# Recurrent memory attention on one core: odd heads' scores earlier, value copies by strip halves, token values after the output product

## The chip, the cores and the metric

The kernel runs on one core of one Trainium2 chip. The metric is the device time of one execution in microseconds (us); lower is better. The engines are PE (TensorE: matmuls, and weight loads that overlap them), DVE (VectorE), ACT (ScalarE), POOL (GpSimd) and SP (SyncE, which here only issues DMAs). Each runs its own instructions in program order and waits on semaphores for the others.

## The reference, cut to what matters

A sequence of 2048 rows of 640 is normalised and cut into 64 segments of 32 rows. Eight memory rows go from segment to segment: what attention puts out for them in one segment is the memory of the next. A feed-forward part (640 to 1728, squared relu, back to 640) follows over all rows.

```python
mem = mem0
for s in range(64):
    h = concatenate([mem, xs[s]])              # 8 + 32 rows of 640
    q, k, v = h @ Wq, h @ Wk, h @ Wv           # 32 heads of 128
    scores = where(mask, q @ k.T * 128**-0.5, -1e9)   # memory rows see all, token rows what is before them
    o = softmax(scores) @ v
    o = o @ Wo                                 # back to 640
    mem, out[s] = o[:8], o[8:]
y = x + out
y = y + (relu(layernorm(y) @ w1 + b1) ** 2) @ w2 + b2
```

## The kernel before

The four attention weights stay in SBUF. `step(b, sp)` does segment s = 4b + sp; its main product has 32 rows, namely the 8 memory rows and the first 24 token rows, which stand side by side in `hTall`. The last 8 token rows of each segment ("tails") need no memory, so their q, k and v products are made ahead, four segments at a time, in small units kept in the list `fill`. One unit is 4 matmuls of 128x512 (or, for the tails' output product, some 6 of 128x320). `run(fill, n)` puts n units at a place in PE's order; the calls of `run(fill, ...)` in `step` are where the kernel fills PE's waits.

The order of work is the order of the code, written out by hand; no scheduler moves anything, and the tile framework adds the semaphore waits. A step goes so on PE:

1. q, k, q, k products (`project`, recorded at line 208 as all products of rows are); between the halves ACT evacuates (L224, L226, L399), DVE transposes (L229, L402) and POOL spreads the memory rows' q into `qz` (L369, L371).
2. `scores(0)`: memory rows' scores of the even half of the heads into the tile `sm`, of which there is one buffer; `soft1` takes the maximum (DVE, L421) and the exponential `em` (ACT, L424), `soft2` the reciprocal, the product and the transpose `pTm` (DVE, L430 to L434). "Even" and "odd" stand here for n = 0 and n = 1.
3. First two fifths of the even heads' v product; `token_scores(0)`; the rest, then its copy to `v` (ACT, L500).
4. Two fifths of the odd heads' v product, `scores(1)`, `token_scores(1)`, the rest of the odd v product (copy at L516), one fill unit.
5. `token_values(s - 1)`: probabilities of the segment before times its values for the token rows, 32 + 8 small matmuls (L350, L355) into the first 256 columns of each of the four banks of `po`.
6. `values(0)` and `values(1)`: the memory rows' value products, 16 + 4 matmuls each (L443, L448), into the columns from 256 on; `values_out`: DVE copies n = 0 (L215), ACT n = 1 (L217) into the last 8 columns of each row of `oT`.
7. Row transposes of the coming block where there are any (list `win`, L185), two fill units; softmax of the token scores on DVE, ACT and POOL (L531 to L546).
8. The output product `wo_rounds` into `pw` (L240, 64 matmuls in 16 rounds, over the 8 memory columns of this segment and 24 token columns of segment s - 2), `wo_out` (ACT copy `otmp`, L247, DVE sum `o`, L248), `mem_to_hT` (two DVE transposes into `hTall`, L314): the next step can start.
9. `token_out(s - 1)`: ACT copies the token values to `oT` (L360), POOL keeps the tail rows (L362); the store of s - 2 (SP); five fill units; `tails_in` (POOL, L318); all remaining fill units; the token probabilities' transposes for the next step.

In `po` the first matmul with `start=True` in a bank opens it; the others add, or write where nothing is yet. Head p of `oT` is p = 16 n + 4 g + j, with strip g of the value products in bank g of `po`. A round of the output product takes its rows so:

```python
                    p = h // 8 * 16 + kh * 8 + h % 8      # h is the round, kh = 0, 1
```

Of the kernel before, what the change touches and what calls it, by code (L numbers as in the profile page):

```python
# [16 lines left out]
def kernel(  # L17
# [19 lines left out]
    M = A_mem0.shape[1]  # L37
    SEG = 32
# [4 lines left out]
    DC = D // 128  # L43
# [5 lines left out]
    NK = SEG + M  # L49
# [25 lines left out]
    wv = wts.tile([128, DC * HE], BF16)  # L75
# [19 lines left out]
    for g in range(G):  # L95
        r = slice(32 * g, 32 * g + 32)
# [101 lines left out]
    def proj(w, by, lhs, n, ps, c0, c1):  # L198

        if by == "columns":  # L200
            wr = w[:].rearrange("p (c g j n k e) -> p c n k g j e", c=DC, g=G, n=2, j=4, k=4)
        elif by == "half":
            wr = w[:].rearrange("p (c k j n e) -> p c n k j e", c=DC, k=G, n=2, j=4)
        else:
            wr = w[:].rearrange("p (c k n f) -> p c n k f", c=DC, k=G, n=2)
        for c in range(c0, c1):
            for k in range(4):
                nc.tensor.matmul(ps[32 * k:32 * k + 32, :], lhsT=lhs(c), rhs=wr[:, c, n, k], start=(c == 0), stop=(c == DC - 1))  # L208
# [4 lines left out]
    def evac(dve, out_, in_):  # L213
        if dve:
            nc.vector.tensor_copy(out=out_, in_=in_)  # L215
        else:
            nc.scalar.copy(out=out_, in_=in_)  # L217
# [33 lines left out]
    fill, late, mid, win = [], [], [], []  # L251

    def run(q, n):
        while n > 0 and q:
            q.pop(0)()
            n -= 1
# [78 lines left out]
    def store_main(o, s):  # L335
        for ch in range(2):
            nc.sync.dma_start(out=o_all[s * SEG:s * SEG + HD, ch * DH:(ch + 1) * DH],
                              in_=o[32 * ch:32 * ch + HD, :])

    oTg = oT[:].rearrange("p (n g j) q -> p n g j q", n=2, g=G)  # L340
    back = []

    def token_values(s, v, vt4, po):

        sp = s % 4
        pTk, pTx = back.pop()
        for i in range(HG):
            for g in range(G):
                r = slice(32 * g, 32 * g + 32)
                nc.tensor.matmul(po[:, g, i * 32:(i + 1) * 32], lhsT=v[r, i * E:(i + 1) * E], rhs=pTk[r, i, :],  # L350
                                 start=(i == 0), stop=False, skip_group_check=True)
        for u in range(2):
            for g in range(G):
                r = slice(32 * g, 32 * g + 32)
                nc.tensor.matmul(po[:, g, u * 128:(u + 1) * 128].rearrange("p (j q) -> p j q", q=32)[:, :, 0:TL],  # L355
                                 lhsT=vt4[r, sp, u, :], rhs=pTx[r, u], start=False, stop=True, skip_group_check=True)

    def token_out(s, po):
        for n in range(2):
            nc.scalar.copy(out=oTg[:, n, :, :, 0:SEG],  # L360
                           in_=po[:, :, n * 128:(n + 1) * 128].rearrange("p g (j q) -> p g j q", q=32))
        nc.gpsimd.tensor_copy(out=oTts[s // 4 % 2][:, :, s % 4 * TL:(s % 4 + 1) * TL], in_=oT[:, :, 0:TL])  # L362
# [10 lines left out]
    prev = {}  # L373

    def step(b, sp, v=None):
        s = b * 4 + sp
        last = s == NS - 1
        lhs = rows_of(b, sp)
        ready = v is not None
        if not ready:  # L380
            v = s2.tile([128, EG], BF16, tag="v", name="v")
# [25 lines left out]
        def scores(n):  # L407
            sm = chn.tile([128, 512], F32, tag="ch", name="sm")
            for g in range(G):
                nc.tensor.matmul(sm[32 * g:32 * g + 32, SEG:2 * SEG], lhsT=ident[:, 0:32],  # L410
                                 rhs=bmask[:].rearrange("p j k -> p (j k)"), start=True, stop=False, skip_group_check=True)
            for j in range(4):
                for g in range(G):
                    p = n * 16 + g * 4 + j
                    nc.tensor.matmul(sm[32 * g:32 * g + 32, 0:2 * SEG], lhsT=qz[:, p, :], rhs=kT[:, p, :],  # L415
                                     start=False, stop=(j == 3), skip_group_check=True)
            sms[n] = sm

        def soft1(n):
            mx = s2.tile([128, 1], F32, tag="mx", name="mx")  # L420
            nc.vector.tensor_reduce(out=mx[:], in_=sms[n][:, 0:2 * SEG], op=ALU.max, axis=AX.X, negate=True)  # L421
            em = s2.tile([128, 2 * SEG], BF16, tag="em", name="em")
            zm = s2.tile([128, 1], F32, tag="zm", name="zm")
            nc.scalar.activation(out=em[:], in_=sms[n][:, 0:2 * SEG], func=ACT.Exp, bias=mx[:, 0:1], scale=1.0,  # L424
                                 accum_out=zm[:])
            ems[n], zms[n] = em, zm

        def soft2(n):
            rm = s2.tile([128, 1], F32, tag="rm", name="rm")
            nc.vector.reciprocal(out=rm[:], in_=zms[n][:])  # L430
            pm = s2.tile([128, 2 * SEG], BF16, tag="pmem", name="pmem")
            nc.vector.tensor_scalar(out=pm[:], in0=ems[n][:], scalar1=rm[:, 0:1], scalar2=None, op0=ALU.mult)
            pT = s2.tile([128, 2 * SEG], BF16, tag="pTm", name="pTm")
            nc.vector.transpose(out=pT[:], in_=pm[:])  # L434
            return pT

        def values(n, pT, po):
            c0 = 256 + n * 4 * M
            for j in range(4):
                i = n * 4 + j  # L440
                for g in range(G):
                    r = slice(32 * g, 32 * g + 32)
                    nc.tensor.matmul(po[:, g, c0 + j * M:c0 + (j + 1) * M], lhsT=v[r, i * E:(i + 1) * E],  # L443
                                     rhs=pT[r, j * M:(j + 1) * M], start=(s == 0 and i == 0), stop=False,
                                     skip_group_check=True)
            for g in range(G):
                r = slice(32 * g, 32 * g + 32)
                nc.tensor.matmul(po[:, g, c0:c0 + 4 * M], lhsT=vt4[r, sp, n, :], rhs=pT[r, 32:64],  # L448
                                 start=False, stop=True, skip_group_check=True)

        def values_out(po):
            for n in range(2):
                c0 = 256 + n * 4 * M
                evac(n == 0, oTg[:, n, :, :, SEG:NK], po[:, :, c0:c0 + 4 * M].rearrange("p g (j m) -> p g j m", m=M))

        project("q", wq, qT, 0)
        if not last and not ready:
# [21 lines left out]
        vt4 = vt4s[b]  # L479
# [6 lines left out]
        def token_scores(n):  # L486
            if n == 0:
                for g in range(G):
                    nc.tensor.matmul(skv[32 * g:32 * g + 32, :, M:NK], lhsT=ident[:, 0:32], rhs=mask[:],
                                     start=True, stop=False, skip_group_check=True)  # L490
            for j in range(4):
                for g in range(G):
                    nc.tensor.matmul(skv[32 * g:32 * g + 32, n * 4 + j, :], lhsT=qT[:, n * 16 + g * 4 + j, :],  # L493
                                     rhs=kT[:, n * 16 + g * 4 + j, 0:NK], start=False, stop=(n == 1 and j == 3),
                                     skip_group_check=True)
# [3 lines left out]
            proj(wv, "half", lhs, 0, ps0, 2, DC)  # L499
            nc.scalar.copy(out=v[:, 0:512], in_=ps0[:])  # L500
        if not last:
            pT0 = soft2(0)
        if not ready:
            ps1 = mmtile()
            proj(wv, "half", lhs, 1, ps1, 0, 2)
        if not last:
            scores(1)
        token_scores(1)
        if not ready:
            proj(wv, "half", lhs, 1, ps1, 2, DC)  # L510

        if not last:
            soft1(1)
            pT1 = soft2(1)
        if not ready:
            nc.scalar.copy(out=v[:, 512:1024], in_=ps1[:])  # L516
        run(fill, 10 if ready else 1)
        if ready:
            run(late, 100)
        po = pop.tile([128, G, 512], F32, tag="po", name="po")  # L520
        if s:
            token_values(s - 1, prev["v"], prev["vt4"], po)
        if not last:
            for n, pT in ((0, pT0), (1, pT1)):
                values(n, pT, po)
            values_out(po)
# [24 lines left out]
        o = wo_out(pw)  # L551
        if not last:
            mem_to_hT(o, (s + 1) // 4, (s + 1) % 4)
        if s:
            token_out(s - 1, po)
        if s > 1:
            store_main(o, s - 2)
        if not last:
            run(fill, 5)
            tails_in((s + 1) // 4, (s + 1) % 4)  # L560
        run(mid, 2)
        run(fill, 100)
# [218 lines left out]
    po = pop.tile([128, G, 512], F32, tag="po", name="po")  # L781
# [7 lines left out]
    for t in range(S // NT):  # L789
# [6 lines left out]
        for fc in range(FC):  # L796
            ps = mmtile()
            for c in range(DC):
                if fc < FFULL:
                    nc.tensor.matmul(ps[:], lhsT=w1[:, c, fc * 128:(fc + 1) * 128], rhs=hnT[:, c, :],  # L800
                                     start=(c == 0), stop=(c == DC - 1))
                    continue
                for hh in range(2):
                    nc.tensor.matmul(ps[FREM * hh:FREM * (hh + 1), 0:HT], lhsT=w1[:, c, fc * 128:F],
                                     rhs=hnT[:, c, HT * hh:HT * (hh + 1)], start=(c == 0), stop=(c == DC - 1))
            w = NT if fc < FFULL else HT
            r = rs_[fc % 4]
# [73 lines left out]
```

## Time and profile before

| | us |
|---|---|
| median of 3 runs | 1051.98 (1051.05 to 1052.34) |
| the profiled execution | 1052.44 |
| its span | 1050.6 |
| PE matmul busy | 964.3 |
| DVE busy | 656.6 |
| ACT busy | 536.5 |
| POOL busy | 326.0 |

A row of the timeline gives start, length, engine, line, operation, output and inputs, shape, count and, in brackets, the idle time before it and what ended that. Rows that overlap on PE are pipelined matmuls, whose ends are modelled. A row of the windows view gives a stretch, its length, and for PE, PEld (weight loads), DVE, ACT and POOL the busy time and the count of instructions; then granted clock, DMA share and GB/s.

### The profile page before, as it was taken

To read this page: it belongs to the slowest core of one execution; us is meant where nothing else is said; L and a number is where in the kernel's file an instruction comes from. 1 tells how busy PE (TensorE), PEld (TensorE's weight loads), DVE (VectorE), ACT (ScalarE), POOL (GpSimd) and SP (SyncE) were. 2 spreads that over 40 slices of the span, in tenths; PEclk is the share of its full clock that TensorE was granted. 3 is DMA by queue.
4 is the path that set the end of the run, shared out by engine and by line. 5 is a ranking of instruction groups with operands and counts; after the bars stand their busy time and mean duration, and the time that the engine had idled before them with its cause. 6 is when DMAs were issued, how large, how long until landed. Compare 5 with 4: busy or idle time off the path is not lost.

```text
span 1050.6 us, 56335 instructions
## 1 busy us (share of the span) xinstructions
PE 964.3 (92%) x25671; PEld 562.9 (54%) x25680; DVE 656.6 (62%) x1804; ACT 536.5 (51%) x1225; POOL 326.0 (31%) x866
## 2 busy tenths in 40 slices
PE   4779799989999999999999999999999998899998
PEld 2335456556555555555555555555555554555565
DVE  2245676767676767666767666666676677565442
ACT  2325455556555555555555555555555555534331
POOL 1033333333333323333333333333333333253110
PEclk9979999999999999999999999999999999999999
DMA  8950100000000001000000000000000110512200
GB/s 325 404 185 25 18 10 26 11 21 9 23 17 20 16 14 32 13 21 14 26 14 22 14 26 15 21 14 27 14 21 8 45 33 6 182 59 76 76 26 26
DMA packets 39183, 51.42 MB, mean 49 GB/s; under 512 B 6240, under 2 KB 35040, under 8 KB 37024
## 3 DMA queue, kind: packets, MB, share of 16 engines
q1 hardware_dynamic: 38080, 47.30, 13.6%
q8 instruction: 200, 3.28, 1.3%
q14 instruction: 39, 0.32, 0.1%
q0 software_dynamic: 320, 0.26, 0.1%
q10 hardware_dynamic: 544, 0.26, 0.1%
HBM read 38.37 MB, written 9.44 MB: 46 GB/s over the span
## 4 chain that ended last, share of the span: by engine, by line
PE 75%; DVE 10%; DMA 5%; issue 4%; ACT 4%; POOL 0%; SPq 0%; ACTq 0%; DVEq 0%; POOLq 0%
PE ps L208 41%; PE pw L240 14%; PE y L832 5%; PE ps L800 5%; DVE hTall L314 3%; DVE o L248 3%; DMA xt<-in_A_x_dram 3%; ACT otmp L247 3%; PE po L443 2%; PE sm L415 2%; PE po L350 1%; PE ps L240 1%; PE ps L493 1%; DMA wq<-in_B_w_dram 1%; DMA vt<-vt_d 1%
## 5 line engine op out<-in xcount | busy, mean ns | idle before, releaser
L208 PEld LDWEIGHTS <-hTall 128*32 128x32 bf16 x7680 | 188.6, 96 | 221.1 <-DVE hTall L314 62.4
L208 PE MATMUL ps<-wq,hTall 128*32 128x512 bf16 x2520 | 158.5, 380 | 35.4 <-DVE hTall L314 34.9
L208 PE MATMUL ps<-wv,hTall 128*32 128x512 bf16 x2520 | 170.0, 379 | 0.7 <-ACT v L500 0.7
L240 PE MATMUL pw<-wo,oT 128*32 128x320 bf16 x4224 | 157.4, 300 | 1.9 <-DVE pTt L564 1.2
L208 PE MATMUL ps<-wk,hTall 128*32 128x512 bf16 x2520 | 157.9, 379 | 0.0
L224 ACT ACTIVATE row<-ps 128x512 bf16<-128x512 f32 x156 | 91.9, 601 | 87.0 <-PE ps L208 84.4
L240 PEld LDWEIGHTS <-oT 128*32 128x32 bf16 x4224 | 111.3, 97 | 45.3 <-DVE oT L215 13.7
L543 POOL TENSOR_TENSOR pkt<-ek,rk 128x64 bf16<-128x64 bf16 x64 | 18.8, 294 | 368.0 <-DVE rk L541 368.0
L229 DVE STREAM_TRANSPOSE qT<-row 128x512 bf16<-128x512 bf16 x128 | 90.0, 704 | 48.2 <-ACT row L224 48.1
L226 ACT CAST row<-ps 128x512 bf16<-128x512 f32 x115 | 65.8, 596 | 36.1 <-PE ps L208 36.1
L318 POOL COPY kT<-kTt 128x1024 bf16<-128x1024 bf16 x64 | 74.6, 1165 | 13.7 <-DVE kTt L229 13.7
L208 PEld LDWEIGHTS <-hTt 128*32 128x32 bf16 x1920 | 51.0, 99 | 42.7 <-issue 7.5
L369 POOL COPY qz<-qT 128x96 bf16<-128x96 bf16 x126 | 33.4, 265 | 122.8 <-DVE qT L229 121.7
L360 ACT CAST oT<-po 128x512 bf16<-128x512 f32 x128 | 68.7, 589 | 1.6
L248 DVE TENSOR_TENSOR o<-pw,otmp 64x320 bf16<-64x320 f32 x66 | 31.8, 482 | 60.3 <-ACT otmp L247 60.3
L229 DVE STREAM_TRANSPOSE kT<-row 128x512 bf16<-128x512 bf16 x65 | 46.0, 708 | 29.6 <-ACT row L226 29.6
L247 ACT COPY otmp<-pw 64x320 f32<-64x320 f32 x66 | 27.9, 422 | 69.6 <-PE pw L240 69.5
L832 PE MATMUL y<-wq,wk 128*128 128x320 bf16 x416 | 61.0, 299 | 0.1
L539 DVE TENSOR_REDUCE zk<-ek 128x8 f32<-128x320 bf16 x64 | 31.1, 486 | 41.8 <-ACT ek L535 41.8
L399 ACT CAST row<-ps 128x256 bf16<-128x256 f32 x126 | 40.7, 375 | 29.6 <-PE ps L208 29.6
L535 ACT ACTIVATE ek<-tk 128x320 bf16<-128x320 f32 x64 | 30.1, 471 | 44.6 <-DVE tk L533 44.6
L424 ACT ACTIVATE em<-sm,mx 128x64 bf16<-128x64 f32 x126 | 40.4, 320 | 24.3 <-DVE mx L421 24.3
(113 smaller groups left out, 1656.1 us busy)
## 6 DMA issues: line engine op xcount, KB each, us to landing
wv<-in_A_Wv_dram SPq DMA_DIRECT2D x5, 1024.0 KB
wq<-in_A_Wq_dram SPq DMA_DIRECT2D x5, 1024.0 KB
wk<-in_A_Wk_dram SPq DMA_DIRECT2D x5, 1024.0 KB
wo<-in_A_Wo_dram SPq DMA_DIRECT2D x4, 1280.0 KB
vt<-vt_d SPq DMA_DIRECT2D x60, 64.0 KB
xt<-in_A_x_dram SPq DMA_DIRECT2D x20, 160.0 KB
vt_d<-row SPq DMA_DIRECT2D x22, 128.0 KB
wq<-in_B_w_dram SPq DMA_DIRECT2D x1, 2080.0 KB
```

What stands on the lines that cost most here:

```text
L208: nc.tensor.matmul(ps[32 * k:32 * k + 32, :], lhsT=lhs(c), rhs=wr[:, c, n, k], start=(c == 0), stop=(c == DC - 1))
L224: nc.scalar.mul(out=row, in_=ps, mul=scale)
L226: nc.scalar.copy(out=row, in_=ps)
L229: nc.vector.transpose(out=dst[:, n * 16:(n + 1) * 16, 0:32], in_=row.rearrange("p (h e) -> p h e", e=32))
L240: nc.tensor.matmul(pw[32 * j:32 * j + 32, 0:DH], lhsT=lhs(p), rhs=wov2[:, head(p), ch], start=(h == 0), stop=(h == 15))
L247: nc.scalar.copy(out=tmp[0:64], in_=pw[64:128, 0:DH])
L248: nc.vector.tensor_tensor(out=o[0:64], in0=pw[0:64, 0:DH], in1=tmp[0:64], op=ALU.add)
L318: nc.gpsimd.tensor_copy(out=kT[:, :, SEG:2 * SEG].rearrange("p h (j k) -> p h j k", k=TL), in_=k.unsqueeze(2).to_broadcast([128, H, 4, TL]))
L360: nc.scalar.copy(out=oTg[:, n, :, :, 0:SEG], in_=po[:, :, n * 128:(n + 1) * 128].rearrange("p g (j q) -> p g j q", q=32))
L399: nc.scalar.copy(out=row[:, u * 256:(u + 1) * 256], in_=ps[:, u * 256:(u + 1) * 256])
L800: nc.tensor.matmul(ps[:], lhsT=w1[:, c, fc * 128:(fc + 1) * 128], rhs=hnT[:, c, :], start=(c == 0), stop=(c == DC - 1))
L832: nc.tensor.matmul(y[:, hh, 0:DH], lhsT=f1T[:, fc, k * 128:(k + 1) * 128], rhs=w2[:, fc, cs], start=(fc == 0), stop=False, skip_group_chec ...
```

## The change

- `scores(1)` and `soft1(1)` move up, ahead of the whole odd v product; the even heads' last transpose (`soft3`) goes behind them, `token_scores(1)` follows, and the odd v product runs unbroken.
- Two fill units in place of one stand ahead of the value products.
- `token_values(s - 1)` moves from ahead of the value products to behind the output product, two fill units after it; `token_out(s - 1)` goes behind it, and the store of s - 2 ahead of both. Four fill units follow in place of five. The value products now open the banks of `po` in every step, the token values only in the last.
- `values_out` splits by strips: DVE copies strips 0 and 1 of both n, ACT strips 2 and 3, where before DVE copied n = 0 and ACT n = 1 of all strips.

```diff
-    def token_values(s, v, vt4, po):
+    def token_values(s, v, vt4, po, first=True):
...
-                                 start=(i == 0), stop=False, skip_group_check=True)
+                                 start=(first and i == 0), stop=False, skip_group_check=True)
...
         def soft2(n):
+            return soft3(soft2a(n))
+
+        def soft2a(n):
...
+            return pm
+
+        def soft3(pm):
             pT = s2.tile([128, 2 * SEG], BF16, tag="pTm", name="pTm")
...
-                                     rhs=pT[r, j * M:(j + 1) * M], start=(s == 0 and i == 0), stop=False,
+                                     rhs=pT[r, j * M:(j + 1) * M], start=(i == 0), stop=False,
...
         def values_out(po):
-            for n in range(2):
-                c0 = 256 + n * 4 * M
-                evac(n == 0, oTg[:, n, :, :, SEG:NK], po[:, :, c0:c0 + 4 * M].rearrange("p g (j m) -> p g j m", m=M))
+            for h in range(2):
+                gs = slice(2 * h, 2 * h + 2)
+                evac(h == 0, oTg[:, :, gs, :, SEG:NK],
+                     po[:, gs, 256:256 + 8 * M].rearrange("p g (n j m) -> p n g j m", n=2, m=M))
...
         if not last:
-            pT0 = soft2(0)
+            pm0 = soft2a(0)
+            scores(1)
+            soft1(1)
+            pT0 = soft3(pm0)
+        token_scores(1)
         if not ready:
             ps1 = mmtile()
-            proj(wv, "half", lhs, 1, ps1, 0, 2)
+            proj(wv, "half", lhs, 1, ps1, 0, DC)
         if not last:
-            scores(1)
-        token_scores(1)
-        if not ready:
-            proj(wv, "half", lhs, 1, ps1, 2, DC)
-
-        if not last:
-            soft1(1)
             pT1 = soft2(1)
...
-        run(fill, 10 if ready else 1)
+        run(fill, 10 if ready else 2)
...
-        if s:
+        if last:
             token_values(s - 1, prev["v"], prev["vt4"], po)
-        if not last:
+        else:
             for n, pT in ((0, pT0), (1, pT1)):
                 values(n, pT, po)
             values_out(po)
...
-        if s:
-            token_out(s - 1, po)
         if s > 1:
             store_main(o, s - 2)
+        if s:
+            if not last:
+                run(fill, 2)
+                token_values(s - 1, prev["v"], prev["vt4"], po, False)
+            token_out(s - 1, po)
         if not last:
-            run(fill, 5)
+            run(fill, 4)
             tails_in((s + 1) // 4, (s + 1) % 4)
```

## The prediction

> **What bounds the kernel now.** I read the page first: how full TensorE is, and what the chain that ended last is made of.
>
> ```profile
> span 1050.6 us, 56335 instructions
> ...
> PE 964.3 (92%) x25671; PEld 562.9 (54%) x25680; DVE 656.6 (62%) x1804; ACT 536.5 (51%) x1225; POOL 326.0 (31%) x866
> ...
> q8 instruction: 200, 3.28, 1.3%
> ```
>
> PE is busy 92% of the span, but that share hides a loop: each step's memory output is the next step's input. So I went on to the chain of waits in order of time for two neighbouring steps (start, length, what).
>
> ```profile
> 500.65 4.50 PE ps L208 x80
> ...
> 509.57 2.28 PE pw L240 x64
> ...
> 513.63 4.50 PE ps L208 x80
> ...
> 521.65 0.35 issue
> ...
> 526.93 4.50 PE ps L208 x80
> ```
>
> A step runs from its q product (L208) to the next one's: 12.98 us for the first, 13.30 for the second. Its last part, from the end of the output product (509.57 + 2.28 = 511.85) over otmp, o and the hTall transposes to the next q product, is 1.78 us of ACT and DVE work that no PE order shortens. The rest is PE in program order with a few handovers. The second step holds one thing more, 0.35 us put down to "issue". The third view is the timeline of all engines in the first, clean step.
>
> ```profile
> 505.58 0.27 POOL L369 COPY qz<-qT 128x96 bf16<-128x96 bf16 x1 [1.43 <-DVE qT L229]
> 505.61 0.77 DVE L402 STREAM_TRANSPOSE kT<-row 128x256 bf16<-128x256 bf16 x2
> ...
> 505.76 1.25 PE L208 MATMUL ps<-wv,hTall 128*32 128x512 bf16 x20
> ...
> 505.94 0.21 ACT L424 ACTIVATION_READ_ACCUMULATOR em<-sm,mx 128x1 f32 x1
> ...
> 506.63 0.59 ACT L500 CAST v<-ps 128x512 bf16<-128x512 f32 x1 [0.48 <-PE ps L208]
> ...
> 507.49 0.31 ACT L424 ACTIVATE em<-sm,mx 128x64 bf16<-128x64 f32 x1 [0.27 <-DVE mx L421]
> ...
> 507.98 0.58 ACT L516 CAST v<-ps 128x512 bf16<-128x512 f32 x1
> ...
> 508.09 0.37 PE L350 MATMUL po<-pTk,v 32*128 32x32 bf16 x32
> ...
> 508.38 0.48 PE L443 MATMUL po<-pTm,v 32*128 32x8 bf16 x16
> 508.40 0.25 DVE L434 STREAM_TRANSPOSE pTm<-pmem 128x64 bf16<-128x64 bf16 x1
> ...
> 508.73 0.26 PE L443 MATMUL po<-pTm,v 32*128 32x8 bf16 x16
> ...
> 508.83 0.19 PE L448 MATMUL po<-pTm,vt 32*128 32x32 bf16 x4
> ...
> 509.11 0.29 DVE L215 CAST oT<-po 128x128 bf16<-128x128 f32 x1 [0.46 <-PE po L448]
> ...
> 509.43 0.27 ACT L217 CAST oT<-po 128x128 bf16<-128x128 f32 x1 [0.87 <-DVE oT L215]
> ...
> 509.45 2.36 PE L240 MATMUL pw<-wo,oT 128*32 128x320 bf16 x64
> ...
> 511.64 1.68 PE L208 MATMUL ps<-wq,hTt 128*32 128x512 bf16 x28
> ...
> 512.37 1.07 ACT L360 CAST oT<-po 128x512 bf16<-128x512 f32 x2
> ```
>
> Two handovers stand on the path. The odd heads' value product (the second L443 group) starts at 508.73, 0.08 after the odd pTm is done (508.40 + 0.25 = 508.65); the token value products at 508.09 only fill that wait. And the output product starts at 509.45, 0.05 after the DVE copy of the even heads ends at 509.40; the ACT copy of the odd heads ends later, at 509.70, but the output product's first eight rounds read even heads only, so it hides.
>
> Now the 0.35 us of issue. I asked for counts of PE instructions between such holes, and for the whole steady stretch:
>
> ```profile
> 127.14:844.24 717.09, 680.71 (x20707) 402.74 (x20708) 490.46 (x1370) 402.06 (x963) 237.60 (x679) 1.00 0.07 19
> ```
> ```profile
> 522.00 0.20 PE L448 MATMUL po<-pTm,vt 32*128 32x32 bf16 x4 [0.35 <-issue]
> ```
> ```profile
> 522.00:535.28 13.29, 12.61 (x384) 7.24 (x384) 9.24 (x25) 7.52 (x18) 4.17 (x12) 1.00 0.03 7
> 614.23:627.57 13.35, 12.66 (x384) 7.11 (x384) 9.49 (x26) 7.53 (x18) 4.28 (x12) 1.00 0.03 6
> ```
> ```profile
> 627.58 0.20 PE L443 MATMUL po<-pTm,v 32*128 32x8 bf16 x6 [0.37 <-issue]
> ```
>
> The 54 steps from 127.15 to 844.24 take 717.09 us, 13.28 each. Between one hole and the next stand 384 matmuls and 384 weight loads, 768 = 3 x 256 instructions. Queue q8 brought 3.28 MB in 200 packets; PE's 51,351 instructions over 200 are 257. So a hole is a packet of PE's own instructions that comes late, and it shows only where 256 instructions pass too fast. The fastest 256 are those that end with the value products: 80 of values, 80 of token values, 8 of fill, 24 of v, 32 of token scores, 32 of scores, all from about 506.9 to 508.9: 2.0 us.
>
> What the holes cost: three steps in four are 12.98 without one. Every fourth also transposes x rows ahead of the output product:
>
> ```profile
> 540.18 4.50 PE ps L208 x80
> ...
> 548.53 0.39 PE pt L185 x5
> ...
> 549.46 2.20 PE pw L240 x64
> ...
> 553.46 0.60 PE ps L208 x5
> ```
>
> That is 13.28, with no hole in it. The mean without holes is (3 x 12.98 + 13.28) / 4 = 13.055, so holes take 13.28 - 13.055 = 0.225 us a step, 12 us in 54 steps.
>
> **The change, part by part**, on the clean step's clock.
>
> *Scores ahead of the odd v product.* The same instructions stand between 505.76 and the end of the odd v product, so the latter ends where it did and its ACT copy still ends at 508.56. Moved up by 8 matmuls of the odd v product (20 take 1.08, so 0.43), scores(1) starts at 506.41. Its cover: em of the even heads ends at 506.15, so the one buffer for score tiles is free; the odd kT halves end at 506.38, 0.03 ahead of need, so this cover is thin (gone, it costs what kT is late, some 0.05). em(1) stands behind the v copy on ACT, which ends at 507.22; it starts at about 507.25 instead of 507.49, and pTm(1), 1.16 later (508.65 - 507.49), is done at 508.41. The even pTm, 0.25 on DVE, now waits behind mx(1), and is done long before values(0).
>
> *Token values out of the way, a second fill unit in.* Between the odd v product and values(1), PE loses 32 + 8 token products (508.09 to 508.38, 0.29) and gains one fill unit of 4 matmuls (28 of them run from the output product's end, 511.81, to 513.32, 1.51, so 0.22). PE would be ready at about 508.45 (508.09 + 0.22 + some 0.1 for values(0)), pTm(1) at 508.41; what is late next is the odd v copy, 508.56. values(1) starts at 508.61 (the 0.05 of the oT handover) instead of 508.73: gain 0.12.
>
> *Copies by strip halves.* As built, the ACT copy still waits for the DVE copy in every one of the 63 steps (the rows they write in oT interleave now). And the output product's first round reads strips of both halves (its second weight pair waits for ACT), where before it read the even heads only. So it starts not 0.05 after the DVE copy but 0.05 after the ACT copy: 509.70 - 509.40 = 0.30 later. Queued behind the waiting weight load is all of PE: the loop waits. In the transposing steps PE is busy there until 549.46 anyway, 0.39 longer; the wait hides, and these steps keep most of the 0.12: 13.20.
>
> *Token values behind the output product.* They go into the 1.78 us in which PE waits for hTall. PE work there was 7 units (1.51, idle from 513.32 to 513.63, 0.31); it becomes 6 units and the token products, 1.29 + 0.29 to 0.38, idle 0.1 to 0.2: free, by that idle time (in steps whose units belong to the tail output it is nearly gone; past it up to 0.1 a step). token_out on ACT (1.07) waits now for the token products, some 0.5 later than 512.37, and the oTt and kT copies on POOL follow it; POOL idles 1.43 before its second qz copy, so this hides. The token values' buffer is read 0.5 later too; the next step first writes it at its value products, 7.7 us in (508.38 - 500.65). On SP only the store's place in the program moves, not its order.
>
> A clean step is thus 12.98 - 0.12 + 0.30 = 13.16, slower than before. The mean without holes: (3 x 13.16 + 13.20) / 4 = 13.17.
>
> *The holes.* Taking 80 instructions out of the fast stretch is the gain nobody orders. The fastest 256 now end with the value products and hold 80 of values, 16 of fill, 40 of v, 32 of token scores, 40 of scores, 24 of the even v product and 24 of the first token scores: from about 505.7 to 508.75, 3.1 us instead of 2.0. The packet that came late at 522.00 bounds what is needed:
>
> ```profile
> 518.73:521.99 3.26, 2.92 (x148) 1.71 (x141) 2.04 (x9) 1.99 (x7) 0.51 (x3) 1.00 0.02 5
> ```
>
> That stretch, the 256 instructions ahead of the hole as counted back from it, lasted 3.26 us with the 0.35 of waiting in it. So 3.3 us a packet is surely enough; 3.1 may leave up to 0.2 now and then, where a packet's end falls into the value products (about 80 places of 256). Holes left: 0 to 0.06 a step; I take 0.02. A hole cannot be less than nothing; the upper bound is the 0.225 of today.
>
> Sum: 13.28 - (13.17 + 0.02) = 0.09 us a step, 54 steps, 5 us. The other steps (first, last, feed-forward) I take as unchanged: they wait for DMA or other products. The profiled execution is 1052.44 (span 1050.6), 0.46 above the median 1051.98: 1047 against the median.
>
> **Rivals.**
>
> *A, slower: the holes stay.* If a packet's coming late does not depend on how dense the stretch is, or the new order has stretches as dense for it, the 0.225 stays on top of 13.17: 13.395, +0.115 a step, +6 us, 1058. It decides from holes of about 0.11 a step upwards. For it: packets need up to 3.3 us and my densest stretch is 3.1. Against: all holes I looked at end at the same place of 256 and in the fast stretch. The Trainium skill (Runtime: NRT & Kernel Launch, section Instruction fetch mechanics) gives refills in blocks of 256 instructions fetched while the current one runs, and calls crossing a block mostly hidden. By that rule the holes would be something else, and A the result; the trace agrees on the block's size, and disagrees on hidden, with 0.35 us at 522.00.
>
> *B, much faster: the two copies do run side by side.* Both would end near 509.30 on the new clock, the output product start 0.30 earlier, clean steps come to 12.86; 40 steps x 0.30 = 12 us more: 1035. The built waits speak against it. The Trainium skill (PSUM — Partial Sum Buffer, PSUM bank collisions) has two engines read different banks at once without harm, which is what halves by strip allow; by that rule alone B would hold. No row of before shows it: 509.43 follows 509.40.
>
> *C, slower: the window overfills.* If the token products, or token_out behind them on ACT, hold up the next step's q row by over 0.1 us, a step is 13.3 or more: 1053 to 1060. It decides where PE has no idle left before the q product.
>
> **Chances.** Forecast 0.66, A 0.16, B 0.05, C 0.13. The forecast's own range is 1043 to 1051 (0.07 a step either way). The whole range goes up to A's 1058 and C's middle, and leaves B out: 1042 to 1058. A difference of 0.2%, 2.1 us, is about what a measurement of this kernel can tell. Faster by more: most of the forecast and B, 0.64; within: 0.14; slower: 0.22.
>
> **What would show it.** In the profile after: L217 still released by L215; the output product's weight load waiting for ACT, idle 0.3 before it on PE; values(1) released by the odd v copy; no or few "issue" waits at the value products; PE idle before hTall down to 0.1 or 0.2; clean steps of 13.1 to 13.2, all alike. Wrong: ACT and DVE copies side by side; holes as often as before; q products that wait for anything but hTall.

## The result and the profile after

| | before | after |
|---|---|---|
| median, measured side by side | 1052.16 (1051.05 to 1053.84, 4 runs) | 1044.73 (1044.32 to 1044.90, 4 runs) |
| the profiled execution | 1052.44 | 1044.78 |
| its span | 1050.6 | 1043.0 |

The ratio is 0.9927, with a 95% interval of 0.9910 to 0.9945. The forecast was 1047. Two lines of the page of after come first.

```profile
span 1043.0 us, 56466 instructions
...
PE 986.2 (95%) x25680; PEld 558.0 (54%) x25680; DVE 650.4 (62%) x1804; ACT 530.6 (51%) x1225; POOL 323.4 (31%) x866
```

PE is busier than before (986.2 against 964.3) though it does the same work. The 22 us are not work. Matmul ends are modelled and overlap, so a short wait between two matmuls is covered by the modelled end of the first: the 4224 matmuls of the output product take 300 ns each in both profiles, but as a group they are busy for 157.4 us before and 169.5 after. The rest stands in the groups of the fill units. The next view is the chain of waits in order of time for two neighbouring steps of after.

```profile
497.03 4.50 PE ps L208 x80
...
503.11 0.15 PE ps L500 x16
...
505.87 2.52 PE pw L240 x64
...
510.21 4.50 PE ps L208 x80
...
523.38 1.68 PE ps L208 x25
```

Both steps, from q product to q product, take 13.17 to 13.18. Of the 39 steady steps of before that transpose no rows, the shortest take 12.94 to 12.95; only 11 are within 13.01, and the longest takes 13.73. The 12.98 of the prediction's first step is therefore not quite clean. A clean step became longer by 0.22, and the spread is gone: 38 of the 39 take 13.17 to 13.18. The windows view puts that into sums: first the 54 steady steps (the same steps as in the prediction, which start a little later here and end earlier), then the last four steps.

```profile
127.50:839.79 712.29, 698.90 (x20707) 398.08 (x20707) 486.15 (x1370) 396.88 (x963) 235.28 (x678) 1.00 0.07 19
...
839.79:893.80 54.01, 49.04 (x1503) 29.39 (x1503) 39.80 (x115) 28.72 (x70) 20.37 (x56) 1.00 0.07 19
```

The same last four steps in the windows view of before:

```profile
844.24:901.18 56.94, 49.19 (x1503) 29.83 (x1503) 41.38 (x115) 29.45 (x71) 20.75 (x57) 1.00 0.07 18
```

The 54 steps took 717.09 before and take 712.29, 4.80 less. The last four took 56.94 and take 54.01, 2.93 less. With the start (0.35 longer) and the end (0.3 shorter) that makes the difference between the spans (7.6, or 7.7 before rounding).

The timeline of the first of the two steps shows the handovers.

```profile
504.39 0.58 ACT L520 CAST v<-ps 128x512 bf16<-128x512 f32 x1 [0.48 <-PE ps L208]
504.42 0.25 DVE L440 STREAM_TRANSPOSE pTm<-pmem 128x64 bf16<-128x64 bf16 x1
...
505.03 0.26 PE L449 MATMUL po<-pTm,v 32*128 32x8 bf16 x16
...
505.40 0.29 DVE L215 CAST oT<-po 128x128 bf16<-128x128 f32 x1 [0.73 <-PE po L454]
...
505.72 0.27 ACT L217 CAST oT<-po 128x128 bf16<-128x128 f32 x1 [0.75 <-DVE oT L215]
505.74 0.10 PEld L240 LDWEIGHTS <-oT 128*32 128x32 bf16 x2 [0.37 <-DVE oT L215]
505.75 2.65 PE L240 MATMUL pw<-wo,oT 128*32 128x320 bf16 x64
506.04 2.02 PEld L240 LDWEIGHTS <-oT 128*32 128x32 bf16 x62 [0.20 <-ACT oT L217]
...
508.76 0.37 PE L350 MATMUL po<-pTk,v 32*128 32x32 bf16 x32
508.97 0.24 PE L355 MATMUL po<-pTx,vt 32*128 32x32 bf16 x8
509.14 1.05 PE L208 MATMUL ps<-wq,hTt 128*32 128x512 bf16 x16
509.43 1.07 ACT L360 CAST oT<-po 128x512 bf16<-128x512 f32 x2
...
510.21 0.34 PEld L208 LDWEIGHTS <-hTall 128*32 128x32 bf16 x12 [0.52 <-DVE hTall L314]
```

Counted from the step's q product (497.03): the odd value product starts at 8.00, 0.06 after the odd v copy ends at 504.97 and no longer behind pTm; before it was 8.08 (508.73 - 500.65). The output product loads two weights after the DVE copy, then waits until 506.04, 0.05 after the ACT copy. So the delay does not show as a gap on PE: it shows as a group of 64 matmuls that takes 2.65. It ends at 11.37 (505.75 + 2.65 - 497.03). Before, by the same rows, the group took 2.36 and ended at 11.16 (509.45 + 2.36 - 500.65). The window from there to the next q product is 1.81, before 1.82 (the prediction's 1.78 takes the end from the chain, 511.85). The waits of after, summed over the kernel (us in total, times, longest):

```profile
ACT oT L217 <- DVE oT L215: 50.4, 63, 3.9
...
PEld L240 <- ACT oT L217: 9.4, 47, 0.2
```

47 of 63 steps wait 0.2 for the ACT copy: all but the transposing ones. No wait of a PE matmul is put down to "issue" in this view.

### The profile page after: what moved, and what is told of

It is laid out like the page before. It is cut to its first block, busy times and chain, and to the rows that moved or that the text cites. A ratio compares the mean times of both kernels' runs of the same rounds, so it can differ in the third digit from the quotient of the medians.

```text
span 1043.0 us, 56466 instructions
## 1 busy us (share of the span) xinstructions
PE 986.2 (95%) x25680; PEld 558.0 (54%) x25680; DVE 650.4 (62%) x1804; ACT 530.6 (51%) x1225; POOL 323.4 (31%) x866
## 4 chain that ended last, share of the span: by engine, by line
PE 86%; DMA 6%; DVE 3%; issue 2%; ACT 2%; POOL 0%; SPq 0%; DVEq 0%; ACTq 0%; POOLq 0%
PE ps L208 48%; PE pw L240 14%; PE y L839 6%; PE ps L807 5%; PE ps L240 3%; DMA xt<-in_A_x_dram 3%; PE po L449 3%; PE sm L415 2%; DMA wq<-in_B_w_dram 2%; PE ps L500 1%; PE po L350 1%; DVE o L248 1%; DMA vt<-vt_d 1%; ACT otmp L247 1%; PE ps L496 1%
## 5 line engine op out<-in xcount | busy, mean ns | idle before, releaser
L240 PE MATMUL pw<-wo,oT 128*32 128x320 bf16 x4224 | 169.5, 300 | 1.8 <-DVE pTt L571 1.2
L226 ACT CAST row<-ps 128x512 bf16<-128x512 f32 x115 | 68.0, 591 | 36.7 <-PE ps L208 36.0
L318 POOL COPY kT<-kTt 128x1024 bf16<-128x1024 bf16 x64 | 72.0, 1124 | 13.8 <-DVE kTt L229 13.8
L362 POOL COPY oTt<-oT 128x256 bf16<-128x256 bf16 x64 | 25.7, 402 | 101.5 <-ACT oT L360 99.7
```

The costliest lines, as they stand in the source:

```text
L226: nc.scalar.copy(out=row, in_=ps)
L240: nc.tensor.matmul(pw[32 * j:32 * j + 32, 0:DH], lhsT=lhs(p), rhs=wov2[:, head(p), ch], start=(h == 0), stop=(h == 15))
L318: nc.gpsimd.tensor_copy(out=kT[:, :, SEG:2 * SEG].rearrange("p h (j k) -> p h j k", k=TL), in_=k.unsqueeze(2).to_broadcast([128, H, 4, TL]))
```

## The experiments

All times are medians, and the ratios are to the kernel before measured beside each run. The steps are read from the q products of each profiled execution: "clean step" is the length that the shortest steps without row transposes agree on, "mean step" is over the 54 steady steps, "last four" are the steps after them.

| | time | ratio to before (95%) | clean step | mean step | last four |
|---|---|---|---|---|---|
| before | 1052.16 | | 12.95 | 13.28 | 56.94 |
| after | 1044.73 | 0.9927 (0.9910 to 0.9945) | 13.17 | 13.19 | 54.01 |
| scores moved alone | 1051.85 | 0.9993 (0.9982 to 1.0005) | 12.90 | 13.31 | 56.38 |
| halves alone | 1064.33 | 1.0118 (1.0098 to 1.0137) | 13.22 | 13.48 | 57.13 |
| token values moved alone | 1035.86 | 0.9850 (0.9831 to 0.9870) | 12.95 | 13.04 | 53.97 |
| after, copies by n again | 1031.47 | 0.9812 (0.9794 to 0.9831) | 12.89 | 12.99 | 53.44 |
| after, po as two tiles | 1031.39 | 0.9812 (0.9787 to 0.9837) | 12.88 | 12.99 | 53.40 |
| before, shifted by 128 instructions | 1047.93 | 0.9970 (0.9956 to 0.9984) | 12.95 | 13.21 | 55.30 |
| after, window fuller | 1046.02 | 0.9942 (0.9924 to 0.9960) | 13.19 | 13.23 | 54.09 |
| after, shifted by 56 instructions | 1045.27 | 0.9930 (0.9915 to 0.9946) | 13.17 | 13.20 | 54.02 |
| before, last kT copies on ACT | 1052.26 | 0.9996 (0.9982 to 1.0009) | 12.95 | 13.32 | 55.04 |
| copies by n, token_scores(1) later too | 1023.80 | 0.9730 (0.9709 to 0.9751) | 12.74 | 12.88 | 53.05 |

**What do the copies by strip halves cost?** First the changed kernel with the old copies.

```diff
-            for h in range(2):
-                gs = slice(2 * h, 2 * h + 2)
-                evac(h == 0, oTg[:, :, gs, :, SEG:NK],
-                     po[:, gs, 256:256 + 8 * M].rearrange("p g (n j m) -> p n g j m", n=2, m=M))
+            for n in range(2):
+                c0 = 256 + n * 4 * M
+                evac(n == 0, oTg[:, n, :, :, SEG:NK], po[:, :, c0:c0 + 4 * M].rearrange("p g (j m) -> p g j m", m=M))
```

> The changed kernel with the copies of the value products put back to even heads on DVE, odd heads on ACT. My theory: the strip halves cost 0.30 us in every step that has no row transposes, because the output product's first round then waits for both copies; so clean steps fall from 13.17 to 12.87 us, transposing steps stay at 13.22, 40 steps x 0.30 = 12 us: 1032 to 1034 us. Rival, that the late ACT copy is off the path: 1044 to 1046 us.

It took 1031.47, 13 us less than after and half a microsecond under the expected range: the rest of the change alone is worth 1.9%. The timeline of one of its steps:

```profile
497.69 0.29 DVE L215 CAST oT<-po 128x128 bf16<-128x128 f32 x1 [0.74 <-PE po L454]
498.01 0.27 ACT L217 CAST oT<-po 128x128 bf16<-128x128 f32 x1 [0.75 <-DVE oT L215]
498.03 2.02 PEld L240 LDWEIGHTS <-oT 128*32 128x32 bf16 x64 [0.37 <-DVE oT L215]
```

The ACT copy waits for the DVE copy here too, but all 64 weight loads run on from 498.03 in one group: nothing needs the odd half so early.

Then the other way round, the halves alone in the kernel before (the same hunk, reversed).

> The kernel before with only the copies by strip halves. My theory: the output product waits for the ACT copy, which waits for the DVE copy, 0.30 us later in steps without row transposes (about 41 of the 54 steady steps), holes as before: 1061 to 1066 us. Rival, that the later start gives PE's instruction blocks time to come, so that part of the holes hides in the wait: 1054 to 1059 us.

It took 1064.33, as expected. The timeline of one step has the same figure as after: two weight loads, then a wait for ACT.

```profile
517.45 0.27 ACT L217 CAST oT<-po 128x128 bf16<-128x128 f32 x1 [1.43 <-DVE oT L215]
517.47 0.10 PEld L240 LDWEIGHTS <-oT 128*32 128x32 bf16 x2 [0.38 <-DVE oT L215]
...
517.76 2.02 PEld L240 LDWEIGHTS <-oT 128*32 128x32 bf16 x62 [0.20 <-ACT oT L217]
```

A clean step is 13.22, 0.27 longer than the 12.95 of before; the prediction's term was 0.30.

**Why does the ACT copy wait for the DVE copy?** The prediction gave as the reason that the rows they write in `oT` interleave. The rival is that both read one tile, `po`. So `po` became two tiles of two banks, one for strips 0 and 1, one for 2 and 3; what is written in `oT` stayed, except that `token_out` also copies by strip halves (and a tile that only the start of the kernel uses, `pa`, is split in the same way).

```diff
-        po = pop.tile([128, G, 512], F32, tag="po", name="po")
+        po = [pop.tile([128, 2, 512], F32, tag="po%d" % h, name="po%d" % h) for h in range(2)]
...
-                nc.tensor.matmul(po[:, g, c0 + j * M:c0 + (j + 1) * M], lhsT=v[r, i * E:(i + 1) * E],
+                nc.tensor.matmul(po[g // 2][:, g % 2, c0 + j * M:c0 + (j + 1) * M], lhsT=v[r, i * E:(i + 1) * E],
```

> The changed kernel with the four banks of po as two tiles of two banks, so that the ACT copy waits for its value products and no longer for the DVE copy; strip halves stay. My theory: both copies run side by side and end within 0.05 us of each other, the output product starts 0.05 later, clean steps of 12.87 us, 1032 to 1034 us as with copies by heads. Rival 1: the two copies slow each other down in PSUM, each some 0.5 us instead of 0.29: 1040 to 1044 us. Rival 2: the second copy starts no earlier for another reason: 1044 to 1046 us.

It took 1031.39, 13 us less than after. The timeline of one step (the view ends within the weight loads), and the line of the waits that answers to the one of after:

```profile
498.24 0.29 DVE L215 CAST oT<-po 128x128 bf16<-128x128 f32 x1 [0.72 <-PE po L454]
498.29 0.27 ACT L217 CAST oT<-po 128x128 bf16<-128x128 f32 x1 [0.45 <-PE po L454]
498.59 1.49 PEld L240 LDWEIGHTS <-oT 128*32 128x32 bf16 x48 [0.36 <-DVE oT L215]
```
```profile
ACT oT L217 <- PE po L454: 32.5, 63, 4.6
```

The two copies run side by side in all 63 steps, at the lengths that they have one after the other (0.29 and 0.27), although they write the same interleaved rows. So the rows were not the reason; the common tile is. (In the kernel before the two copies wrote rows that do not interleave, and ACT waited for DVE there as well.) It is also what the prediction's rival B needed: the rule of the Trainium skill quoted there (PSUM — Partial Sum Buffer, PSUM bank collisions), that engines may read different banks at once, agrees with these two rows.

**Which edit takes the holes away?** The token values alone, moved in the kernel before, with the fill units of the change.

```diff
-        run(fill, 10 if ready else 1)
+        run(fill, 10 if ready else 2)
...
-        if s:
+        if last:
             token_values(s - 1, prev["v"], prev["vt4"], po)
-        if not last:
+        else:
...
-        if s:
-            token_out(s - 1, po)
         if s > 1:
             store_main(o, s - 2)
+        if s:
+            if not last:
+                run(fill, 2)
+                token_values(s - 1, prev["v"], prev["vt4"], po, False)
+            token_out(s - 1, po)
         if not last:
-            run(fill, 5)
+            run(fill, 4)
```

> The kernel before with only the token values moved behind the output product (and the fill units shared out 2, 2, 2 + 4 as in the changed kernel). My theory: the holes of about 0.35 us at the value products are late blocks of 256 PE instructions, and thinning out the fastest 256 instructions removes them; a clean step stays at 12.98 us since values(1) still waits for the odd pTm at 8.05 us into the step; mean step 13.06 instead of 13.28: 12 us less, 1038 to 1041 us, no issue waits at the value products. Rival, that the holes have another cause and stay: 1050 to 1053 us.

It took 1035.86, less than the expected 1038 to 1041; its mean step was as expected, and the rest came mostly from the last four. The steady steps in the windows view:

```profile
126.00:830.31 704.31, 685.72 (x20708) 399.41 (x20709) 491.25 (x1370) 402.56 (x963) 236.56 (x678) 1.00 0.07 20
```

That is 13.04 a step, and a clean step is 12.95, the same as before: so the 0.24 a step are holes that are gone, and the move itself is worth nothing on the clean step. The scores alone:

```diff
-            pT0 = soft2(0)
+            pm0 = soft2a(0)
+            scores(1)
+            soft1(1)
+            pT0 = soft3(pm0)
         if not ready:
             ps1 = mmtile()
-            proj(wv, "half", lhs, 1, ps1, 0, 2)
-        if not last:
-            scores(1)
+            proj(wv, "half", lhs, 1, ps1, 0, DC)
         token_scores(1)
-        if not ready:
-            proj(wv, "half", lhs, 1, ps1, 2, DC)
```

> The kernel before with only the odd heads' scores moved ahead of the odd v product; token values stay ahead of the value products. My theory: values(1) then waits for the odd v copy instead of the odd pTm, 0.05 us earlier, 13.0 to 12.93 us in a clean step, some 3 us in all; the block ends still fall into the value products, and the 256 instructions ahead of them take as long as before less those 0.05, so the holes stay: 1047 to 1051 us. Rival, that the earlier scores alone thin out the fastest stretch enough to remove the holes: 1037 to 1041 us.

It took 1051.85, no difference, and just above the 1047 to 1051 of the theory. Its waits of PE matmuls in the steady stretch:

```profile
PE po L449 <- issue: 6.3, 17, 0.6
PE po L454 <- issue: 3.0, 4, 1.3
```

A clean step is 12.90, better by 0.05 as the theory had it, but the mean is 13.31 against 13.28: the holes took it all. With the token values out of the way as well, 12.95 becomes 12.89 (copies by n, above), and that counts.

**Is it the place in the program or the place among 256 instructions?** 64 useless matmuls of 128x128 ahead of the whole kernel before move every packet's end by 128 instructions, half a packet.

```diff
+    idle = mmtile()
+    for _ in range(64):
+        nc.tensor.matmul(idle[:, 0:128], lhsT=ident[:], rhs=ident[:], start=True, stop=True)
```

> The kernel before with 64 useless matmuls (128 PE instructions) at the very start, where PE waits for the first loads. Nothing in the steps changes. My theory: holes are at the ends of 256-instruction blocks; in the kernel before the block end falls 480 to 540 instructions into nearly every step, in the value products; 128 instructions more move it to 350 to 410 and 610 to 670, where the 256 instructions ahead of it take longer: most holes go, 12 us less, 1038 to 1042 us. Rival, that holes belong to the value products themselves (a data wait, a buffer): they stay, 1051 to 1054 us.

It took 1047.93, some 3 us less (the ratio is 0.9970), with not one instruction less in a step. That is between the theory and the rival, and in the range of neither. In the timeline the holes have left the value products; these two now stand inside the output product:

```profile
608.27 1.67 PE L240 MATMUL pw<-wo,oT 128*32 128x320 bf16 x42 [0.26 <-issue]
...
662.03 1.40 PE L240 MATMUL pw<-wo,oT 128*32 128x320 bf16 x35 [0.34 <-issue]
```
```profile
608.27:662.03 53.76, 51.02 (x1537) 31.00 (x1536) 36.33 (x102) 29.70 (x72) 17.62 (x50) 1.00 0.06 17
```

Between them stand 1537 matmuls and 1536 weight loads, 12 x 256 instructions within one (the windows row). So a hole sits at one place of a packet, whatever the instruction is there. The traces show it for every hole: with PE's matmuls and weight loads counted in order of start, all 32 waits of PE matmuls on "issue" up to 901 us of before, and all 9 up to 891 us of the shifted kernel, stand at the same place of 256, the 190th. They also fit the packets of q8: the 27 of them in the steady steps of before end 1.24 to 1.60 us after a packet of q8 has landed, while PE's other passes of that place come a median of 3.1 us after one.

The mean step is 13.21, so only 0.07 of 0.24 went, and the rest moved to another dense stretch. In the 39 steps without row transposes of before, the value products (from the end of the odd v copy to the end of the DVE copy) take 1.04 on average where 0.80 is the shortest, and the output product (from there to `otmp`) takes 2.57 where 2.52 is the shortest. In the shifted kernel these means are 0.80 and 2.73: the loss has left the value products and stands in the output product, most of it under modelled ends.

The same question for the changed kernel: its gain could be a lucky place. By count, the 190th place of a packet falls into the value products in 42 of the 54 steady steps of before, but in only 10 of after. 28 matmuls (56 instructions) ahead of the kernel after make that 44.

```diff
+    idle = mmtile()
+    for _ in range(28):
+        nc.tensor.matmul(idle[:, 0:128], lhsT=ident[:], rhs=ident[:], start=True, stop=True)
```

> The changed kernel with 28 useless 128x128 matmuls (56 PE instructions) ahead of everything, so that each packet of 256 PE instructions ends 56 places earlier in the step, in the value products. Theory (holes come where the end of a packet follows a dense stretch, and the new order has no stretch dense enough anywhere): a clean step stays at 13.17, no waits put down to issue on PE at the value products, 1044 to 1046. Rival (the changed kernel only happens to have its packet ends at good places; its densest 256 instructions last about 3.1 us, which leaves some waiting): holes of 0.05 to 0.2 a step come back, issue waits at the value products, 1047 to 1056.

It took 1045.27, as expected, against 1044.73. The steady steps in the windows view:

```profile
126.74:839.33 712.59, 699.02 (x20708) 398.03 (x20709) 486.25 (x1370) 397.27 (x963) 236.68 (x678) 1.00 0.07 19
```

That is 13.20 a step. Step by step against after, one of the 54 is longer by 0.27, at its value products, and no other by more than 0.02. So the new order bears its packets at this place too. Only this one other place was tried.

**Is the window behind the output product full?** One fill unit (0.22) moved from ahead of the value products into the window of after.

```diff
-        run(fill, 10 if ready else 2)
+        run(fill, 10 if ready else 1)
...
-            run(fill, 4)
+            run(fill, 5)
```

> The changed kernel with one fill unit less ahead of the value products and one more behind the output product. My theory: PE had 0.02 us of idle left before hTall is ready, so one unit more (0.22 us) makes PE late for the next q product by 0.2 us in steps with 10 units: gap after the output product 2.02 instead of 1.81 us, 40 steps x 0.2 = 8 us: 1051 to 1054 us. Rival, that PE catches up elsewhere and the handover to the value products gets shorter: 1044 to 1047 us.

It took 1046.02: the rival's range, and not the theory's. The weight load of the q product, in its timeline:

```profile
509.92 1.00 PEld L208 LDWEIGHTS <-hTall 128*32 128x32 bf16 x24 [0.30 <-DVE hTall L314]
```

The wait for hTall shrank from 0.52 to 0.30, by just the unit's 0.22, and a clean step grew by only 0.02: the room was there. In 13 of the 39 steps without row transposes, those whose units belong to the tails' output, the window grew from 1.81 to 1.96, so there it is full. The 0.02 of idle time that the matmul rows of after leave ahead of hTall (509.14 + 1.05 = 510.19) is the model's end, not PE's.

**Where do the 2.9 us of the last four steps come from?** In the table the last four take 53.0 to 54.1 in every kernel in which the token values are moved, and 55.0 to 57.1 in every one in which they aren't. These steps also prepare the feed-forward's first rows: `hn`, a normalised row block on DVE (L638 before, L645 after). All four in before, and one of them beside its neighbour on POOL, by the timeline:

```profile
L638 DVE TENSOR_SCALAR hn<-ht,lnmv,lnrs x4: 462/1226/1271, 858.3 to 901.2; 128x640 bf16<-128x640 bf16 x4
...
886.03 1.36 POOL L318 COPY kT<-kTt 128x1024 bf16<-128x1024 bf16 x1
886.36 1.22 DVE L638 TENSOR_SCALAR hn<-ht,lnmv,lnrs 128x640 bf16<-128x640 bf16 x1
```

And in after:

```profile
L645 DVE TENSOR_SCALAR hn<-ht,lnmv,lnrs x4: 446/519/1271, 853.4 to 893.8; 128x640 bf16<-128x640 bf16 x4
...
880.07 0.52 DVE L645 TENSOR_SCALAR hn<-ht,lnmv,lnrs 128x640 bf16<-128x640 bf16 x1
880.35 1.24 POOL L318 COPY kT<-kTt 128x1024 bf16<-128x1024 bf16 x1
```

(The three numbers are the shortest, middle and longest, in ns.) In after the POOL copy is later, since token_out is, and hn slips in ahead of it in two of the first three steps (0.52); in the other it starts behind the copy and takes 1.27. To see whether the POOL copy is the cause, the kernel before was run with that copy on ACT, in the last four steps only.

```diff
-        nc.gpsimd.tensor_copy(out=kT[:, :, SEG:2 * SEG].rearrange("p h (j k) -> p h j k", k=TL),
-                              in_=k.unsqueeze(2).to_broadcast([128, H, 4, TL]))
+        cp = nc.scalar.copy if 4 * b + sp >= 60 else nc.gpsimd.tensor_copy
+        cp(out=kT[:, :, SEG:2 * SEG].rearrange("p h (j k) -> p h j k", k=TL),
+           in_=k.unsqueeze(2).to_broadcast([128, H, 4, TL]))
```

> The kernel before, with the copy of the tails' k into kT (L318) on ACT instead of POOL for the last four steps only. Before, three of the four hn instructions of the last steps (L638, DVE) took 1.22 to 1.27, each beside such a copy on POOL; the fourth, without one, took 0.46. Theory (DVE's hn is slow because POOL copies at the same time): all four hn take 0.45 to 0.55, ht 0.49 where it was 0.63; those steps get up to 0.7 shorter on DVE, but ACT takes about 1 us more between token_out and the next q row, so the time is anywhere in 1049 to 1053. Rival (hn is slow by its own input or place in the step): three of four stay at 1.2. What tells them apart is hn's length, not the time.

```profile
L639 DVE TENSOR_SCALAR hn<-ht,lnmv,lnrs x4: 434/436/465, 859.3 to 900.5; 128x640 bf16<-128x640 bf16 x4
```

All four hn now take 0.43 to 0.47, so the POOL copy is what slowed them. `ht`, another DVE instruction of these steps, stayed at 0.63, so that part of the expectation was wrong. The last four steps took 55.04, 1.9 less. That is one execution's gain: there the steady steps were longer, 13.32 each, and the medians do not show it (0.9996, from 0.9982 to 1.0009).

The Trainium skill (SBUF — State Buffer, section SBUF: two separate sides) describes a pair of ports that a DVE instruction in a two-port mode and a GpSimd instruction hold in turn, each for a whole instruction, the other one blocked. The trace agrees in the order: in before hn ends at 887.58, 0.19 after the POOL copy that was ahead of it, and in after it is short where it starts first, at 880.07. But 0.19 is less than the 0.43 that hn takes alone, so not all of it was held back, and no run shows in which mode it ran.

The other part of the 2.9 is holes. In before's last four steps the waits of PE matmuls hold 1.9 us of them:

```profile
PE pt L648 <- issue: 0.7, 1, 0.7
...
PE ps L240 <- issue: 0.6, 1, 0.6
PE po L443 <- issue: 0.6, 2, 0.4
```

In after the same view of those steps has none; with the copies on ACT it has 0.9, so of the 1.9 gained there about 1.0 is holes as well, and 0.9 is left for hn. An estimate from these numbers is thus that of the 2.93 some 1.9 were holes, about two thirds, and some 0.9 hn; holes too short for the view (under 0.15) are not in it, and a clean step of after is 0.22 longer besides. That both come with the token values' place is shown by the table.

**A faster version.** In after the odd value product waits for the odd v copy, and the 0.15 of `token_scores(1)` (503.11 in the chain) stand ahead of that v product. With the old copies, they go behind it.

```diff
-        token_scores(1)
         if not ready:
             ps1 = mmtile()
             proj(wv, "half", lhs, 1, ps1, 0, DC)
+        token_scores(1)
```

> The changed kernel with copies by heads and with token_scores(1) behind the odd v product. My theory: the odd v product and its ACT copy end 0.12 us earlier and the value products wait for that copy, so every step is 0.12 us shorter: 1031.5 - 7 = 1024 to 1026 us. Rival 1, that PE has no idle left and the work behind the output product becomes the bound: 1029 to 1032 us. Rival 2, holes come back as 16 + 16 small instructions move into the stretch ahead of the value products: 1027 to 1036 us.

It took 1023.80, just under the expected range, 2.7% less than before and about 2% less than after (1023.80 / 1044.73, which were not measured side by side). A clean step is 12.74, just the 0.15 shorter than 12.89. The chain of waits still shows a hole in it, now among the tails' output units in the window:

```profile
524.39 0.35 issue
```

## Why the prediction was right, and where it was off

- **Bounds.** The reading of before held in the main: a loop with a clean step and, on top, holes. The kernel with token values moved alone took out the holes (0.24 a step, 0.225 forecast) and left the clean step. But "three steps in four are 12.98 without one" was read off too few steps: the clean step is 12.95, and most steps of before are longer than that. The step at 500.65 has a hole too: PE's 189th and 190th instruction of the packet start at 7.82 and 8.02 us into the step, and the wait for pTm hides all of this but 0.03.
- **Scores earlier, token values out: 0.12 forecast, 0.05 measured.** The odd value product starts at 8.05 in a clean step of before and at 8.00 in after; the clean step gains 0.05 by the scores alone, and 0.06, from 12.95 to 12.89, where the token values are out as well. The release was as forecast, the odd v copy. Of the 0.07 too much, 0.03 is the small hole in the 8.08 of the step at 500.65, and 0.03 that the odd v copy ends at 7.94 and not, as before, at 7.91. The scores alone gave the 0.05 and lost it to holes.
- **Halves: +0.30 forecast, 0.28 measured.** In after the output product's group took 2.65 instead of 2.36, +0.29, and the pairs of kernels with and without the halves give 0.28 (13.17 against 12.89) and 0.27 (13.22 against 12.95). Right in place and size. **Wrong was the reason in the parentheses**, "the rows they write in oT interleave": with `po` as two tiles the copies write the same rows and run side by side. The number held because the wait was read from the built order, not from the reason.
- **The clean step: 13.16 forecast, 13.17 measured, partly by luck.** The start was 0.03 too high (12.98 for 12.95), the gain of the scores 0.07 too large and the price of the halves 0.02 too large; these errors all but cancel.
- **Window: free, 0.1 to 0.2 idle.** It cost nothing (1.82 before, 1.81 after); the fuller window shows some 0.2 of real room in most steps and none in the tail output's. The forecast sign "PE idle 0.1 or 0.2" could not be seen in the matmul rows, which show 0.02; only the wait of the weight loads showed it.
- **Holes: 0.02 left.** None are seen in the steady steps; mean 13.19, exactly the forecast's 13.17 + 0.02. The term of -5 us measured -4.80. That 3.1 us for the fastest 256 might leave something came true once in 54 steps of the shifted kernel. The 3.3 us that a packet was said to need is no fixed price, though: in before two of the 190th places stand only 2.38 us apart, at 361.6, so what PE needs between packets stays open. Rival A fell. What the Trainium skill says (Runtime: NRT & Kernel Launch, section Instruction fetch mechanics), that crossing a block is mostly hidden, holds for the order after and not for the one before, which lost 0.24 a step by it.
- **The other steps "unchanged": this is the term that was mis-sized.** The last four gave 2.93 us, beside 4.80 from the 54. The move of token_out was followed on POOL as far as the question whether POOL is late, and "hidden" was the answer. It was not asked whom POOL's copy disturbs while it runs, and the holes of these four steps were not counted, only those of the 54. With the 2.9 taken off, the forecast of 1047 is 1044, against 1044.73 measured.
- **Rival B** (both copies side by side, 1035) was a true description of the kernel with two tiles, at 1031.39: the 12 us given there were 13.3. **Rival C** did not decide: the window held 0.22 more.

## What to carry to other kernels

Read the parts of a change apart: here one edit is worth 16 us, one nothing by itself and 4 beside the first, and one costs 13; the sum is a gain of 7. When small instructions come thick, count them: taking 80 instructions out of the densest 256 was the greater part of the 16 us, where the dearest handover cost 13. When an instruction moves on an engine that idles, ask also what runs beside it at the new place.

## What was not expected of the hardware

- In the kernel before PE waits 0.2 to 0.7 us, 32 times up to 901 us, always at the same place of 256 of its own instructions and not at a fixed instruction: 128 useless instructions at the start of the kernel made it some 3 us faster (0.9970, 0.9956 to 0.9984).
- DVE's hn takes 0.43 to 0.47 alone and 1.22 to 1.27 when POOL's copy of 128x1024 started ahead of it; started ahead of the copy it takes 0.52.
